# Order of work in a fused mLSTM and gated MLP kernel: the plan of the second product's steps, the place of the decay, and the joins of the first chunk

## The chip, the cores and the metric

The kernel runs on one core of a Trainium2 chip. The metric is the device time of one execution in microseconds. A core has TensorE (PE, matmuls; PEld is its weight load), VectorE (DVE), ScalarE (ACT), GpSimd (POOL) and SyncE (SP, which issues nearly all transfers here). Each works through its own queue in order; semaphores tie the queues together.

## The reference

An mLSTM cell runs over 768 time steps for 4 batches of 8 heads with a head dimension of 40. Its output, 3072 tokens of 320 values, goes through a two-layer block with a gate `h cos(h)`.

```python
# for each step t, with m the running maximum of the gates
C = f_stab * C + i_stab * outer(v_t, k_t)
n = f_stab * n + i_stab * k_t
y_t = sigmoid(o_t) * (C @ q_t) / max(|n . q_t|, 1)
# x = y as (3072, 320)
h = x @ w_in                     # w_in 320 x 2048
out = (h * cos(h)) @ w_out       # w_out 2048 x 320
```

## The kernel before

**Tiles.** Time is cut into 6 chunks of 128 steps. A cell `n` is one batch of one chunk (24 cells, `c, b = divmod(n, 4)`). A cell computes decay exponents E (8 heads of 128 x 128), scores, weighted scores, values, and a normalized result that is written transposed into xT. A chunk of xT, 512 tokens over the four batches, then goes through w_in.

**The loop.** `both_parts(c, b)` (line 976) runs the MLP of chunk c beside cell `n = 4(c + 1) + b`, the next chunk's cell of the same batch. It holds two *slots*, `8c + 2b` (first half) and `8c + 2b + 1` (second half). Each slot makes one `Up` (line 617): 8 + 4 matmul instructions into two PSUM tiles, then per tile `near` (ScalarE, line 639), `rest` (VectorE, line 642), `sin` (ScalarE, line 647) and `gate` (VectorE, lines 654 and 659). `ps_u` has two buffers, both used by one Up: the next Up can't begin before the gates have read the last one's tiles. In the first half the cell's scores, weighing, values and normalizing lie around the Up, in the second half the seam (the transposes of the result or, in later chunks, the state's product) and the state.

**w_out.** In chunk 0 `down_first(p)` (line 823) multiplies directly. From chunk 1 on a *step* `(c, s, p, parted)` adds piece p (of 8) to the sums of half s of chunk c. A parted step (`in_parts`, line 729) makes seven products P1 to P7 of 128 x 160 from sums of gate tiles, `S` (GpSimd, line 723), and differences of w_out, `T` (line 696); a whole step (`whole`) makes eight matmul instructions of 128 x 320. The step with p = 7 ends a sum: `put_together` (one ScalarE copy and seven VectorE ops, lines 759 and 765), or `whole_out` (two copies, line 752), and then the result transfers. `plan` (lines 679 to 690) is a hand-written table that says in which slot each step runs; `down(T)` (line 783) carries out a slot's steps, whole ones first, and `sums(T)` makes their S a slot ahead. The sums lie in `ps_o`, four PSUM banks in turn; a group takes three (`sums_room`, line 773), and (1,0) and (1,1) together four.

**Order on the engines.** The program order is written out by hand (`manual_schedule`), and each engine keeps it. The lines that the change and the prediction touch:

- `decay_exponents(n)` (373): VectorE subtraction (375) and GpSimd select (376); `decay(n)` (384): ScalarE's exponential. The exponential and the sine need different tables; `sin_next` (963) runs the sine on one element, so that its table is loaded early.
- `parts` and `join` (132, 143): the weights arrive as 64-bit floats. `parts` makes two ScalarE passes (138, 140) into the buffers wt and wm, two of each in turn; `join` makes three VectorE ops (144, 146, 148) and an integer add (149), on GpSimd or, in the first cells, on VectorE. In chunk 0 each block joins three pieces of w_in for the next block and two pieces of w_out.
- `turn_blocks(n)` (414): VectorE's 32 x 32 transposes, for cells from `TURNED = 7` on; before that TensorE turns (`turn`).
- `values_turned`, `normalize_turned` (490 to 522): PSUM tiles hp in `ps_a`, two buffers; VectorE's line 519 reads them, and the second half's `seam` (596) takes the same buffers.
- `first_cells` (839): gates and the first four cells, and the first w_in pieces.

In the first half of a block with c > 0 the program order before the change is: Up, scores, near, rest, weigh, rest, sin and gate twice, decay_exponents(n + 1), then (for a slot that ends a sum) the steps with put_together, then decay(n + 1), values, normalize. The second half: sin_next, sums, Up, seam, near, rest, sin and gate, state, the slot's steps, turn_blocks of the next cell.

Of the kernel before, what the change touches and what calls it, by code (L numbers as in the profile page):

```python
# [29 lines left out]
def kernel(  # L30
# [22 lines left out]
    B, H, S, D = q.shape  # L53
    C = 128
# [328 lines left out]
    def decay(n):  # L383
        nc.scalar.activation(out=Es[n], in_=Es[n], func=AF.Exp, scale=-1.0)  # L384
# [294 lines left out]
    def put(T, *steps):  # L679
        plan.setdefault(T, []).extend(steps)  # L680

    for p in range(NP):
        put(9 + p, (1, 0, p, IN_PARTS))
        put((9, 11, 13, 15, 17, 17, 18, 18)[p], (1, 1, p, WHOLE))
        put((19, 19, 20, 21, 21, 22, 23, 24)[p], (2, 0, p, IN_PARTS))
        for c in range(2, NC):
            if c > 2:
                put(8 * c + 5 + p // 2, (c, 0, p, IN_PARTS))
            put(8 * c + 9 + p // 2, (c, 1, p, WHOLE if c == NC - 1 and p == NP - 1 else IN_PARTS))
# [39 lines left out]
    def in_parts(c, s, p):  # L729
        P1, P2, P6, P5, P3, P4, P7 = po[c, s]  # L730
        g, S, T = gs[c, p, s], sg[c, s, p], Ts[p]
        w0, w1 = (w_out_sb[:, 2 * p + e] for e in range(2))
        last = p == NP - 1 or (c, s, p + 1, WHOLE) in plan[LAST]

        for out, a, w, first in ((P1, g[:, 0:C], w0[:, lo], True), (P2, g[:, 2 * C:3 * C], w1[:, lo], False),
                                 (P6, S[:, 1], T[:, 1], False), (P7, S[:, 2], T[:, 2], c > 1),
                                 (P5, S[:, 0], T[:, 0], True), (P3, S[:, 3], w1[:, hi], False),
                                 (P4, g[:, 3 * C:4 * C], T[:, 3], False)):
            product(out, a, w, first and p == 0, last)

    def whole(c, s, p, b, sums, alone=False):
# [8 lines left out]
    def whole_out(c, b, sums):  # L750
        o = p2.tile([128, DM], FP, name="o_sb", tag="o_sb")
        nc.scalar.copy(out=o, in_=sums)
        result(c, b, o)
# [19 lines left out]
    def sums_room(c, s):  # L773

        t = [ps_o.tile([128, 3 * DH + 32], FP, name="po", tag="o") for _ in range(3)]
        po[c, s] = [t[i // 3][:, ts(i % 3, DH)] for i in range(7)]
        if c == 1:

            t.append(ps_o.tile([128, 3 * DH + 32], FP, name="po", tag="o"))
            po[c, s][6] = t[2][:, DM:DM + DH]  # L780
            po[c, 1] = [x[:, 0:DM] for x in t[2:]]

    def down(T):

        rests = []
        steps = sorted(plan[T], key=lambda step: (step[3], step[:3]))
        for c, s, p, parted in steps:
            if p == 0 and (c, s) not in po:
                sums_room(c, s)
        for c, s, p, parted in steps:  # L790
            end = p == NP - 1
            if parted:
                in_parts(c, s, p)
                if end:
                    o2 = put_together(c, s)
                    rests.append(lambda c=c, s=s, o2=o2: [result(c, 2 * s + b, o2[:, b]) for b in range(2)])
            else:
                for b in range(2):
                    whole(c, s, p, b, po[c, s][b])
                if end:  # L800
                    rests.append(lambda c=c, s=s: [whole_out(c, 2 * s + b, po[c, s][b]) for b in range(2)])
            spare.append(gs.pop((c, p, s)))
        return rests

# [34 lines left out]
    def first_cells():  # L839
        nc.vector.memset(nil, 0.0)  # L840
        gates_in()
        nc.scalar.copy(out=ident_b, in_=ident)
        load(0, "qk")
        later_gates_in()
        load(1, "qk")
        load(0, "v")
        load_o(0, (0, 1))
        load(2, "qk")
        load_E(0)
        load_E(1)  # L850
        warm(7)
        gates_first()
        later_fills()
        wall_in(0, 0, pmu)
        wall_in(0, 1, psum_o())
        spread(0, 0)
        gates_first_out()
        decay_exponents_half(0, 0)
        turn(0)
        turn_out(0, False)  # L860
        gates_sums()
        spread(0, 1)
        decay_exponents_half(0, 1)
        decay(0)
        weigh_k(0)
        load_E(2)
        load(1, "v")
        load(3, "qk")
        load(2, "v")
        load_E(3)  # L870
        load_o(0, (2, 3))
        load(3, "v")
        pieces.extend(weights_in(0))
        wall_in(1, 0, psum_o())
        wall_in(1, 1, psum_o())
        gates_less_sums()
        spread(1, 0)
        decay_exponents_half(1, 0)
        scores(0)
        gates_maxima()  # L880
        turn(1)
        weigh(0)
        turn_out(1, False)
        sigmoid(0, slice(0, 2))
        spread(1, 1)
        decay_exponents_half(1, 1)
        gates_exponents()
        decay(1)
        weigh_k(1)
        values(0)  # L890
        normalize(0)
        scores(1)
        turn(2)
        turn_out(2, False)
        warm(2)
        seam(0)
        weigh(1)
        seam_out(0)
        state(0)
        load_E(B)  # L900
        load(B, "qk")
        decay_exponents(2)
        decay(2)
        weigh_k(2)
        gates_exp()
        values(1)
        outs.append((0, weights_out(0)))
        load(B, "v")
        load_o(1, (0,))
        load_E(B + 1)  # L910
        normalize(1)
        scores(2)
        turn(3)
        seam(1)
        weigh(2)
        turn_out(3)
        seam_out(1)
        decay_exponents(3)
        gates_diagonal()
        values(2)  # L920
        decay(3)
        weigh_k(3)
        state(1)
        scores(3)
        weigh(3)
        pg = gates_turn()
        warm(5)
        values(3)
        join(*parts(*pieces.pop(0)))
        sigmoid(0, slice(2, 4))  # L930
        gates_keep(*pg)
        pieces.extend(weights_in(1))
        load(B + 1)
        outs.extend((p, weights_out(p)) for p in range(1, 3))
        load_o(1, (1, 2, 3))
        normalize(2)
        warm(5)
        seam(2)
        seam_out(2)
        second = parts(*pieces.pop(0))  # L940
        normalize(3)
        warm(4)
        seam(3)
        join(*second, nc.vector)
        decay_exponents(B)
        seam_out(3)
        join(*parts(*pieces.pop(0)), nc.vector)
        load_E(B + 2)
        state(2)
        state(3)  # L950

        nc.scalar.activation(out=spot, in_=spot, func=AF.Exp)
# [23 lines left out]
    def both_parts(c, b):  # L976
# [25 lines left out]
        up.rest(1)  # L1002
        if c == 0 and not begin:
            weigh(n)
        if begin:
            decay_exponents(n + 1)
        for e in range(2):
            up.sin(e)
            up.gate(e)
        if more and c > 0:  # L1010
            decay_exponents(n + 1)
        if n == TURNED:
            turn_gates(n)
# [7 lines left out]
        if pieces:  # L1021
            h = parts(*pieces.pop(0))
        rests = []
        ends = any(step[2] == NP - 1 for step in plan.get(slot, ()))
        if ends:
            rests = down(slot)
        if begin or more and c > 0:
            decay(n + 1)
        elif more:
            decay_by_bias(n + 1)  # L1030
        if 0 < slot <= NP:
            down_first(slot - 1)
# [4 lines left out]
        if cell:  # L1037
            if n < TURNED:
                load(n + 2)
                if not begin:  # L1040
                    values_kept(n)
                values(n)
                normalize(n)
                if h:
                    join(*h)
            else:
                values_turned(n)
                if h:
                    join(*h)

                normalize_turned(n)
                if n + 2 < N:
                    load(n + 2, "q")
                last_in(n)
                if n + 2 < N:
                    load(n + 2, "bkv")
            if TURNED <= n + 2 < N:
                load_G(n + 2)
            if n + 3 < N:
                load_E(n + 3)  # L1060
            if b == B - 2 and c + 2 < NC:
                load_o(c + 2)
            fade(n)
            if n + 1 == TURNED:
                turn_blocks(n + 1)
        h = ()
        sin_next()
        if pieces:
# [10 lines left out]
            seam_out(n)  # L1079
        if cell and n < TURNED:  # L1080
            state(n)
        if h:
            join(*h)
        for e in range(2):
            up.sin(e)
            up.gate(e)
        if n >= TURNED and cell:
            state(n)
        if b == B - 1 and 0 < c < NC - 2:
            sigmoid(c + 2)  # L1090
            sin_next()
        if more:
            weigh_k(n + 1)
        if c == 1 and b < B - 1:
            two_differences(2 * b + 2)
        if pieces:
            join(*parts(*pieces.pop(0)))
        if c == 0:
# [67 lines left out]
```

## Time and profile before

| | |
|---|---|
| median of 3 runs | 537.48 us (532.47, 537.48, 537.7) |
| the profiled execution's own time | 532.62 us |
| its span in the profile | 530.9 us |
| TensorE busy | 518.6 us |
| VectorE busy | 404.5 us |
| ScalarE busy | 264.7 us |
| GpSimd busy | 210.0 us |
| TensorE's idle time in 40 to 120 us | 3.0 us (80.00 less 76.99) |
| TensorE's idle time in 208 to 222 us | 0.7 us (14.00 less 13.32) |
| TensorE's idle time in 265 to 300 us | 1.7 us (35.00 less 33.26) |

Times in the profile are microseconds from the start of the span. A row of a timeline gives start, duration, engine, line, operation, output and inputs, and how many instructions it merges; in brackets stands the idle time before it and what ended it. Chunk 0's blocks run from about 36 us (slot 0) to 128 us, slot 1 begins at 47.5, slot 2 at 59.2, slot 4 at 83.3, slot 6 at 107.0. Slot 16 begins at 204.8, slot 18 at 224.4, slot 24 at 280.8. An idle time counts toward the end only if the engine is the bound at that place.

### The profile page before, as it was taken

Reading aid. Unit: us, or ns where it says so; the run is one execution under the profiler, and the core shown is the slowest. Engines: PE = TensorE matmul, PEld = TensorE weight load, DVE = VectorE, ACT = ScalarE, POOL = GpSimd, SP = SyncE. Lnnn points to the kernel's source line nnn. Section 1 sums busy time; section 2 is a strip of 40 time slices with the busy share of each in tenths; the row PEclk is TensorE's granted clock in tenths of the full one; section 3 lists DMA queues with packets and bytes.
Section 4 is the critical chain, followed back from the end, with each engine's and each line's share of the span. In section 5 each row is a group of like instructions: output and inputs, shape, how many; then the busy total and the mean of one; then the engine's idle time right before and its main releaser. Section 6 shows DMA issues by size and latency. Waiting matters only on the chain.

```text
span 530.9 us, 10605 instructions
## 1 busy us (share of the span) xinstructions
PE 518.6 (98%) x3855; PEld 343.8 (65%) x3855; DVE 404.5 (76%) x864; ACT 264.7 (50%) x418; POOL 210.0 (40%) x409
## 2 busy tenths in 40 slices
PE   9999999999999999999999999999999999999996
PEld 6865566655565656556665577577577576757596
DVE  5878768889789998978999988988878864325253
ACT  3789696766543637543556363356353332313210
POOL 6522433333827532122521643532533524344350
PEclk9999999999999999999999999999999999999999
DMA  9989998932463475356276355366354100000000
GB/s 139 217 205 240 221 237 183 212 77 66 130 143 73 97 150 116 111 123 146 54 148 147 83 118 116 85 136 143 86 107 83 41 11 29 2 1 26 0 27 25
DMA packets 134860, 57.80 MB, mean 109 GB/s; under 512 B 70248, under 2 KB 130872, under 8 KB 134808
## 3 DMA queue, kind: packets, MB, share of 16 engines
q1 hardware_dynamic: 134664, 56.93, 48.2%
q8 instruction: 30, 0.49, 0.4%
q0 software_dynamic: 96, 0.18, 0.2%
q14 instruction: 22, 0.18, 0.1%
q10 hardware_dynamic: 48, 0.02, 0.0%
HBM read 50.76 MB, written 6.34 MB: 108 GB/s over the span
## 4 chain that ended last, share of the span: by engine, by line
PE 73%; DVE 8%; SPq 6%; ACT 6%; DMA 4%; issue 2%; POOL 0%; DVEq 0%; ACTq 0%; POOLq 0%
PE po L727 29%; PE pup L631 26%; PE pup L634 8%; SPq L332 4%; PE hp L496 3%; PE po L823 3%; PE ps L453 2%; DMA bits<-in_moe_w_in_dram 2%; PE hp L490 2%; DVE n L642 1%; SPq L129 1%; DMA qs<-in_q_dram 1%; PE pu L596 1%; ACT n L639 1%; ACT wt L138 1%
## 5 line engine op out<-in xcount | busy, mean ns | idle before, releaser
L631 PE MATMUL pup<-xT,w_in_sb 128*128 128x512 f32 x384 | 175.4, 599 | 3.2 <-DVE g L654 1.8
L639 ACT ACTIVATE n<-pup 128x512 int32<-128x512 f32 x96 | 51.8, 590 | 149.0 <-PE pup L634 149.0
L642 DVE SCALAR_TENSOR_TENSOR n<-pup,n 128x512 f32<-128x512 f32 x96 | 63.2, 685 | 80.0 <-ACT n L639 79.7
L631 PEld LDWEIGHTS pup<-xT,w_in_sb 128*128 128x128 f32 x384 | 69.6, 190 | 76.8 <-issue 65.5
L647 ACT ACTIVATE n<-n 128x512 f32<-128x512 f32 x96 | 59.5, 631 | 41.1 <-DVE n L642 41.1
L376 POOL TENSOR_SCALAR_AFFINE_SELECT E<-E 128x1024 f32<-128x1024 f32 x19 | 20.7, 1091 | 147.3 <-DVE E L375 139.8
L727 PE MATMUL po<-T,sg 128*128 128x160 f32 x426 | 69.4, 299 | 0.0
L727 PEld LDWEIGHTS po<-T,sg 128*128 128x128 f32 x426 | 61.7, 190 | 0.0
L634 PE MATMUL pup<-xT,w_in_l 64*128 64x512 f32 x192 | 54.7, 641 | 0.6 <-DVE w_in_l L149 0.6
L723 POOL TENSOR_TENSOR sg<-g 128x128 f32<-128x128 f32 x66 | 30.4, 460 | 53.6 <-PE po L727 40.9
L723 POOL TENSOR_TENSOR sg<-gg 128x128 f32<-128x128 f32 x66 | 30.6, 464 | 28.7 <-PE po L727 27.6
L634 PEld LDWEIGHTS pup<-xT,w_in_l 64*128 64x128 f32 x192 | 14.7, 184 | 37.2 <-issue 33.4
L384 ACT ACTIVATE E<-E 128x1024 f32<-128x1024 f32 x21 | 22.2, 1057 | 32.3 <-POOL E L376 28.6
L727 PE MATMUL po<-w_out_sb,g 128*128 128x160 f32 (+1 forms) x180 | 38.3, 341 | 0.0
L823 PE MATMUL po<-w_out_sb,g 128*128 128x320 f32 x128 | 36.6, 439 | 0.7 <-POOL w_out_sb L149 0.7
L414 DVE STREAM_TRANSPOSE t<-qs 128x512 f32<-128x512 f32 x34 | 35.1, 1112 | 0.4
L727 PEld LDWEIGHTS po<-w_out_sb,g 128*128 128x128 f32 x180 | 27.8, 189 | 11.0 <-issue 6.8
L727 PE MATMUL po<-w_out_sb,gg 128*128 128x160 f32 (+1 forms) x168 | 34.0, 329 | 0.0
L659 DVE SCALAR_TENSOR_TENSOR g<-pup,n 128x256 f32<-128x256 f32 x82 | 31.1, 417 | 2.1 <-ACT n L647 0.8
L459 DVE TENSOR_TENSOR E<-ps,E 128x512 f32<-128x512 f32 x48 | 30.7, 680 | 2.5 <-ACT E L384 2.1
L453 PEld LDWEIGHTS ps<-t,t 40*128 40x128 f32 (+1 forms) x384 | 25.4, 188 | 9.5 <-issue 8.9
L659 DVE SCALAR_TENSOR_TENSOR gg<-pup,n 128x256 f32<-128x256 f32 x78 | 29.8, 418 | 2.1 <-ACT n L647 1.2
(171 smaller groups left out, 854.1 us busy)
## 6 DMA issues: line engine op xcount, KB each, us to landing
E<-M_d SPq DMA_DIRECT2D x22, 512.0 KB
bits<-in_moe_w_in_dram SPq DMA_DIRECT2D x40, 128.0 KB
bits<-in_moe_w_out_dram SPq DMA_DIRECT2D x8, 640.0 KB
room<-G_d SPq DMA_DIRECT2D x34, 128.0 KB
ks<-in_k_dram SPq DMA_DIRECT2D x24, 160.0 KB
vs<-in_v_dram SPq DMA_DIRECT2D x24, 160.0 KB
out_dram<-o SPq DMA_DIRECT2D x18, 160.0 KB
o<-in_o_gate_dram SPq DMA_DIRECT2D x68, 40.0 KB
```

The lines of the kernel that those rows point to most:

```text
L414: nc.vector.transpose(out=dst.rearrange("r p (t x) -> r p x t", x=T4), in_=src.rearrange("r p (x d) -> r p x d", x=T4)[:, :, :, 0:32])
L453: nc.tensor.matmul(ps[j][:, p], kT[r, p], qT[r, p], start=True, stop=True)
L459: nc.vector.tensor_tensor(out=w, in0=pss[n][j], in1=w, op=OP.mult)
L631: nc.tensor.matmul(pu, w_in_sb[:, i, ts(block(f2, e), 128)], x(i), start=(i == 0), stop=False)
L634: nc.tensor.matmul(pu, w_in_l[r, f2], x(NK, r), start=False, stop=True)
L639: nc.scalar.activation(out=self.n[e], in_=self.pu[e], func=AF.Copy, bias=0.25)
L642: nc.vector.scalar_tensor_tensor(out=self.n[e].bitcast(FP), in0=self.pu[e], scalar=0.25, in1=self.n[e], op0=OP.add, op1=OP.subtract)
L647: nc.scalar.activation(out=r, in_=r, func=AF.Sin, scale=TWO_PI_DOWN)
L659: nc.vector.scalar_tensor_tensor(out=gs[c, f2, s][:, ts(e, W)], in0=self.pu[e][:, ts(s, W)], scalar=TWO_PI, in1=n[:, ts(s, W)], op0=OP.mul ...
L723: engine.tensor_tensor(out=S[:, i], in0=x, in1=y, op=op)
L727: nc.tensor.matmul(out, g, w, start=start, stop=stop, skip_group_check=True)
L823: nc.tensor.matmul(po[0][b], gs[0, f // 2, f % 2][:, ts(b, C)], w_out_sb[:, f], start=(f == 0), stop=(f == NF - 1))
```

## The change

Five edits; no arithmetic is altered.

1. The plan: whole step (1,1,7) moves from slot 18 to 19, and the steps of (2,0) shift, so that first halves (even slots) from 16 to 24 hold one step each and the second halves 17, 19, 21 and 23 hold two.
2. `in_parts` multiplies in the order P1, P2, P6, P5, P3, P4, P7, where P7 stood fourth. `sums_room` is called when a step needs it, not ahead of all of a slot's steps, and a whole sum's output copies follow at once.
3. `late`: in a block with c > 0 whose first half has a single step and that step ends a sum (slots 16 and 24), decay_exponents(n + 1) and decay(n + 1) move to the second half, behind the state, with one more `sin_next`.
4. Chunk 0: decay_exponents(n + 1) of the first block goes behind the gates; the second half's first join goes behind the gates; turn_blocks(7) goes from the end of a first half to the second half, between its two joins of w_in.
5. `first_cells`: decay_exponents(4) goes behind the third join of w_in.

```diff
-        put((9, 11, 13, 15, 17, 17, 18, 18)[p], (1, 1, p, WHOLE))
-        put((19, 19, 20, 21, 21, 22, 23, 24)[p], (2, 0, p, IN_PARTS))
+        put((9, 11, 13, 15, 17, 17, 18, 19)[p], (1, 1, p, WHOLE))
+        put((19, 20, 21, 21, 22, 23, 23, 24)[p], (2, 0, p, IN_PARTS))
...
-                                 (P6, S[:, 1], T[:, 1], False), (P7, S[:, 2], T[:, 2], c > 1),
-                                 (P5, S[:, 0], T[:, 0], True), (P3, S[:, 3], w1[:, hi], False),
-                                 (P4, g[:, 3 * C:4 * C], T[:, 3], False)):
+                                 (P6, S[:, 1], T[:, 1], False), (P5, S[:, 0], T[:, 0], True),
+                                 (P3, S[:, 3], w1[:, hi], False), (P4, g[:, 3 * C:4 * C], T[:, 3], False),
+                                 (P7, S[:, 2], T[:, 2], c > 1)):
...
         for c, s, p, parted in steps:
+            end = p == NP - 1
             if p == 0 and (c, s) not in po:
-                sums_room(c, s)
-        for c, s, p, parted in steps:
-            end = p == NP - 1
+                sums_room(c, s if c > 1 else 0)
...
-                    rests.append(lambda c=c, s=s: [whole_out(c, 2 * s + b, po[c, s][b]) for b in range(2)])
+                    for b in range(2):
+                        whole_out(c, 2 * s + b, po[c, s][b])
...
         join(*second, nc.vector)
-        decay_exponents(B)
         seam_out(3)
         join(*parts(*pieces.pop(0)), nc.vector)
+        decay_exponents(B)
...
-        if begin:
-            decay_exponents(n + 1)
         for e in range(2):
             up.sin(e)
             up.gate(e)
-        if more and c > 0:
+        ends = any(step[2] == NP - 1 for step in plan.get(slot, ()))
+        late = more and ends and len(plan[slot]) == 1
+        if begin or more and c > 0 and not late:
             decay_exponents(n + 1)
...
-        if begin or more and c > 0:
+        if begin or more and c > 0 and not late:
             decay(n + 1)
-        elif more:
+        elif more and c == 0:
             decay_by_bias(n + 1)
...
-            if n + 1 == TURNED:
-                turn_blocks(n + 1)
...
-        if h:
-            join(*h)
         for e in range(2):
             up.sin(e)
             up.gate(e)
+        if h:
+            join(*h)
         if n >= TURNED and cell:
             state(n)
+        if late:
+            decay_exponents(n + 1)
+            decay(n + 1)
+            sin_next()
...
         if c == 1 and b < B - 1:
             two_differences(2 * b + 2)
+        if n + 1 == TURNED:
+            turn_blocks(n + 1)
         if pieces:
             join(*parts(*pieces.pop(0)))
```

More of the change, by code (lines that the diff above doesn't have):

```diff
@@ L1023, in both_parts @@
         rests = []
-        ends = any(step[2] == NP - 1 for step in plan.get(slot, ()))
         if ends:
             rests = down(slot)
-        if begin or more and c > 0:
+        if begin or more and c > 0 and not late:
             decay(n + 1)
-        elif more:
+        elif more and c == 0:
             decay_by_bias(n + 1)
```

## The prediction

> **What bounds the kernel now.** I read the page first (busy shares), then the table by stretches of the span, then who waited for whom, then TensorE's timeline for its gaps, and last VectorE, ScalarE and GpSimd around each gap.
>
> ```profile
> span 530.9 us, 10605 instructions
> PE 518.6 (98%) x3855; PEld 343.8 (65%) x3855; DVE 404.5 (76%) x864; ACT 264.7 (50%) x418; POOL 210.0 (40%) x409
> ```
> ```profile
> 40.00:120.00 80.00, 76.99 (x456) 47.41 (x455) 65.00 (x125) 62.74 (x110) 28.47 (x30) 1.00 0.85 194
> 120.00:208.00 88.00, 88.00 (x677) 52.98 (x675) 80.08 (x157) 47.62 (x68) 43.54 (x79) 1.00 0.48 109
> 300.00:524.00 224.00, 224.00 (x1614) 156.01 (x1614) 145.93 (x337) 80.59 (x128) 90.33 (x198) 1.00 0.27 62
> ```
> The second number of a row is TensorE's busy time: from 120 to 208 us and from 300 to 524 us it has no gap, at a granted clock of 1.00. The change removes no matmul, so only gaps can be won. Those it aims at are these (bracket: idle time before, and who ended it):
>
> ```profile
> 41.13 1.13 PE L634 MATMUL pup<-xT,w_in_l 64*128 64x512 f32 x4 [0.55 <-DVE w_in_l L149]
> 47.52 3.70 PE L631 MATMUL pup<-xT,w_in_sb 128*128 128x512 f32 x8 [0.32 <-DVE g L654]
> 59.23 3.67 PE L631 MATMUL pup<-xT,w_in_sb 128*128 128x512 f32 x8 [0.66 <-DVE g L654]
> 65.08 4.57 PE L823 MATMUL po<-w_out_sb,g 128*128 128x320 f32 x16 [0.22 <-POOL w_out_sb L149]
> 83.32 3.67 PE L631 MATMUL pup<-xT,w_in_sb 128*128 128x512 f32 x8 [0.20 <-DVE g L654]
> 89.17 4.58 PE L823 MATMUL po<-w_out_sb,g 128*128 128x320 f32 x16 [0.23 <-POOL w_out_sb L149]
> 106.95 3.67 PE L631 MATMUL pup<-xT,w_in_sb 128*128 128x512 f32 x8 [0.62 <-DVE g L654]
> 112.79 4.57 PE L823 MATMUL po<-w_out_sb,g 128*128 128x320 f32 x16 [0.22 <-POOL w_out_sb L149]
> 219.43 0.51 PE L596 MATMUL pu<-vs,kw 128*40 128x41 f32 x16 [0.68 <-DVE room L519]
> 280.77 3.70 PE L631 MATMUL pup<-xT,w_in_sb 128*128 128x512 f32 x8 [1.17 <-DVE g L659]
> 295.88 0.51 PE L596 MATMUL pu<-vs,kw 128*40 128x41 f32 x16 [0.58 <-DVE room L519]
> ```
> The three L823 rows matter most for chunk 0: right behind the wait for a gate comes one for the joined piece of w_out. Two engines share the blame there, and shortening the first wait alone moves nothing. How that piece comes about in slots 3 and 4 (rows of GpSimd, ScalarE and VectorE):
>
> ```profile
> 82.62 1.27 POOL L149 TENSOR_TENSOR w_in_sb<-wt,wm 128x512 int32<-128x512 int32 x1 [3.28 <-DVE wt L148]
> 83.92 0.80 ACT L138 ACTIVATE wt<-bits 128x640 f32<-128x640 f32 x1 [2.37 <-POOL w_in_sb L149]
> 85.15 0.49 DVE L144 TENSOR_SCALAR wt<-wt 128x640 f32<-128x640 f32 x1
> 87.58 1.54 POOL L149 TENSOR_TENSOR w_out_sb<-wt,wm 128x640 int32<-128x640 int32 x1 [1.36 <-DVE wt L148]
> ```
> ScalarE's copy of the w_out piece waited 2.37 us for GpSimd's add of the w_in piece, whose buffers (two in turn) it takes.
>
> **The change, part by part** (times are those of the profiled execution).
>
> **Plan of w_out, chunk 2.** Same 28 steps, moved between slots. Up of slot 24 waited 1.17 for slot 23's gates, because one step (2.10) lay between Up 23 and it; now two lie there (4.00, from the two-step slots), 1.9 more, so 1.17 goes and some 0.7 is left over. What pays is slot 18, with one whole step (eight matmuls, 2.27) instead of 4.5, and 20, 22 with one as before. In slot 18 the first gates ended 3.8 after the start of the ScalarE copy (229.03 to 232.8); scores 0.89, 2.27 and values 1.61 cover 4.77 after Up. No wait: 0. **Gain 1.17.**
>
> **Late decay** (one step that ends seven sums: slots 16 and 24). VectorE's subtraction E (213.97 to 215.10) stood before the seven ops of put_together and normalize; L519 freed the bank for the seam 0.68 and 0.58 late. E moves behind the state, 1.13 of VectorE, so L519 comes 1.13 earlier: both waits go. **Gain 0.68 + 0.58.** What queues behind it: on VectorE, turn_blocks starts at 224.46 as before. On GpSimd, the select moves with it, and in slot 25 the kw product and the eight sums of slot 26 stand behind it: select to 302.8, kw 0.72, then 0.46 each to 307.1, where TensorE wants the second step's first sum at 307.9. 0. On ScalarE, E's exponential waits for the select: select ends 225.77 (224.46 + lag 0.22 + 1.09), exponential, sine table and its one-element op took 2.54 from there to the next copy (216.38 to 218.92): 228.31; Up 18 wants it at 228.35 (229.03 less 0.68). In slot 26: 305.29 against 304.51, 0.8 late, where the gates have 2.6 to spare (308.9 to 311.50). 0, bounds -0 and +0.4 (one more table load of 1.28 in front, less the 0.9 to spare in slot 18). The two added one-element ops (0.20) run while ScalarE idles: 0. No transfer moves here.
>
> The Trainium skill, "ScalarE: Activation LUTs", section "What ACT_TABLE_LOAD costs", speaks against this part: it puts a switch at 2.66 us, 1.28 of load and 1.38 of drain. The row of the sine's load here is 1.28 (217.52) and the next op starts 0.01 later, so no drain shows; by the page the copy of slot 18 would be 1.3 late, 0.44 of it on TensorE, and the sum below would be 0.44 higher. I take the row.
>
> **P7 last, sums_room later, whole_out at once.** Same matmuls. S[2] is needed 0.8 later, S[0], S[3] and P4's g 0.3 earlier; no L727 matmul waits in the trace, and sums lie a slot ahead. In slot 19 P7 needs the bank of the first output copy: copies 0.73 for two right after the whole step, P7 comes 1.8 after it. The two result transfers (160 KB each) move by a slot, past one block's loads on SP; SP waited 15.7 for all such copies without holding TensorE. Were ScalarE busy at that moment, P7 would wait for the copies alone, 0.73. I take 0.
>
> **First cells.** E(4), 1.13 on VectorE, moves behind the third join: w_in_l is ready 2.4 earlier (a neighbouring GpSimd select and kw stretched L146 to 1.07 there), so 0.55 goes. E(4)'s select then ends about 41.1, and its exponential started at 41.51 for ScalarE's own queue: 0. In slot 0 E(5) goes behind the gates: 0.32 goes. TensorE is 0.87 earlier into slot 1, but ScalarE, which sets slot 1 (its copy at 54.24 came 2 us behind Up), only 0.34, the wait it had for VectorE at 45.17.
>
> **Chunk 0, joins behind the gates.** VectorE's steps by start to start, slot 3: rest 1.21, state 0.69, join 1.65, gates 1.21, second join 1.46, w_out join 2.28, then GpSimd 1.69 with lag. Old order: 78.93 to 89.12. New: gates 80.83, join 82.04 to 83.66, GpSimd's add ends 85.10 instead of 83.89, ScalarE's copy 85.13 to 85.93, so the w_out join starts at 85.97 instead of 85.15: the gates no longer lie over that chain, only the second join does. Cost 0.82 at 89.17, less some 0.1 of GpSimd overlap: **+0.7**. Slot 2, the same less the 0.34: **+0.3**; and there Up also waits about 1 us for w_in_sb, so 0.66 isn't won. The w_out join also issues the transfer of the piece three further on, as much later; that piece is turned into floats a block on: 0. Slots don't add: ScalarE's copy at 70.75 waited for a DMA, which anchors slot 3.
>
> Slot 5: TensorE comes 0.7 late, ScalarE's copy at 101.64, rest at 102.25 instead of 102.63 (turn_blocks, 1.94, no longer before it). But turn_blocks now stands between the joins: -0.38 + 1.94 - 0.2 (no GpSimd neighbour for L146) = **+1.35** at 112.79. That replaces the +0.7, and since TensorE has no gap behind 118 it stays to the end. Bounds: -2.35 (all of 0.55, 0.32, 0.66, 0.20, 0.62 won) and +4.0 (the three add up, 0.82 + 0.82 + 1.26, and L146 stretched from 0.70 to 1.07 three times).
>
> **Sum:** -1.17 - 0.68 - 0.58 + 1.35 = -1.08. The profiled execution took 532.62 (span 530.9 and 1.7 around it): **531.5**. The three runs shown are 537.48, 532.47, 537.7; the profiled one is like the lowest, the median 4.86 above. Two of three stood above, so I forecast the median there: 537.48 - 1.08 = **536.4**.
>
> **Rivals.** (1) Everything is won: the copy of the w_out piece doesn't come later, chunk 0 loses all five waits: -2.43 - 2.35 = -4.78, 532.7 on the median. For it: VectorE idles 2.6 to 2.75 before each odd slot's rest. Against: the 2.37 wait above. (2) Slower: in chunk 0 each later GpSimd add hands its delay on, w_in buffer to ScalarE copy to w_out join to L823. At +4.0 the whole is +1.6, 539.1; it decides once chunk 0 costs over 2.43. For it: three L823 rows already wait for GpSimd. Against: the anchor at 70.75. (3) The change wins nothing late: the bank or ScalarE holds slots 17 to 26 as before, only 1.17 comes: +0.2, 537.7. Against: 1.13 moved exceeds both waits.
>
> **How the numbers follow.** Chances: forecast 0.52, (1) 0.20, (2) 0.18, (3) 0.10. About 1% (5.4 us) is what a measurement of this kernel can tell from no change, and no case reaches it alone; the level of the runs can. A median that falls on the lower level (0.3) with a gain is 531.5 or less, faster by over 1%: 0.3 x 0.72, with 0.05 for a gain I don't see: 0.27. Slower by over 1% needs a chunk 0 cost of 7.8 or a wait that the trace doesn't show: 0.13. Within: 0.60. Range: from (1) on the lower level, 527.8 (given as 528), to (2) on the upper with 1 us for a wait not seen, 540.
>
> **What would show it.** Right: no wait before the seams of slots 17 and 25 and before Up 24; E and its select behind the state in slots 17 and 25 only; ScalarE's copy of slot 18 within 0.2 of Up's end; L823 of slots 2, 4 and 6 waiting 0.7 to 1.0 for w_out_sb instead of 0.22, the last of them about 1.3 later; Up 2 waiting for w_in_sb. Wrong: those L823 no later than before (then rival 1), a gap behind 118 us, or a wait of Up 19 for gates.

## The result and the profile after

| | before | after |
|---|---|---|
| median of 20 runs | 533.09 us (531.52 to 537.7) | 531.35 us (529.09 to 536.19) |
| ratio, 95% interval | | 0.9963, 0.994 to 0.9986 |
| profiled execution, span | 532.62, 530.9 us | 532.54, 530.8 us |

The changed kernel is faster by 0.37% (0.14 to 0.6%): about 2.0 us of 533.09, between 0.75 and 3.2. That is within 1%. The forecast gain of 1.08 lies in that interval; the forecast time, 536.4, is 5.0 above the measured median.

The two profiled executions took nearly the same time, for reasons that cancel. The start of each Up on TensorE, from the two timelines, shows it:

| from, to | before | after | difference |
|---|---|---|---|
| span's start to Up 0 | 36.03 | 37.56 | +1.53 |
| Up 0 to Up 7 (chunk 0) | 82.88 | 83.87 | +0.99 |
| Up 7 to Up 27 | 192.52 | 189.99 | -2.53 |
| Up 27 to the last matmul | 215.40 | 215.40 | 0.00 |

The first row comes from a clock that sank before any edited code ran: from 14 to 16 us the two are level to 0.03, by 19 us the changed one is 1.55 behind (more below). The second and third are mainly the change: dearer in chunk 0, cheaper behind it; both hold waits for transfers too, which vary from execution to execution. First the page of the changed kernel and its table by stretches (TensorE's busy time is the second number of a row).

```profile
span 530.8 us, 10591 instructions
PE 519.4 (98%) x3855; PEld 345.3 (65%) x3855; DVE 406.9 (77%) x864; ACT 264.5 (50%) x420; POOL 212.9 (40%) x409
```
```profile
40.00:120.00 80.00, 75.86 (x411) 46.49 (x417) 66.31 (x121) 62.02 (x108) 29.61 (x30) 1.00 0.85 192
120.00:208.00 88.00, 88.00 (x736) 53.68 (x721) 79.22 (x158) 47.18 (x71) 43.37 (x78) 1.00 0.46 106
208.00:222.00 14.00, 14.00 (x133) 8.13 (x131) 12.16 (x31) 5.20 (x10) 0.68 (x2) 1.00 0.56 141
265.00:300.00 35.00, 35.00 (x319) 23.14 (x318) 32.28 (x74) 18.65 (x27) 11.33 (x22) 1.00 0.59 137
```
From 208 to 222 and from 265 to 300 us TensorE has no gap left (0.7 and 1.7 before). From 40 to 120 us its idle time rose from 3.0 to 4.1. Its timeline says where:

```profile
62.49 1.98 PE L631 MATMUL pup<-xT,w_in_sb 128*128 128x512 f32 x4 [1.50 <-POOL w_in_sb L149]
...
67.38 4.57 PE L825 MATMUL po<-w_out_sb,g 128*128 128x320 f32 x16 [0.88 <-POOL w_out_sb L149]
...
91.07 4.58 PE L825 MATMUL po<-w_out_sb,g 128*128 128x320 f32 x16 [0.27 <-POOL w_out_sb L149]
...
112.42 1.13 PE L634 MATMUL pup<-xT,w_in_l 64*128 64x512 f32 x4 [0.62 <-POOL w_in_l L149]
...
115.31 4.57 PE L825 MATMUL po<-w_out_sb,g 128*128 128x320 f32 x16 [0.87 <-POOL w_out_sb L149]
...
221.59 0.51 PE L596 MATMUL pu<-vs,kw 128*40 128x41 f32 x16
...
281.64 3.60 PE L631 MATMUL pup<-xT,w_in_sb 128*128 128x512 f32 x8
...
295.99 0.51 PE L596 MATMUL pu<-vs,kw 128*40 128x41 f32 x16
```
No Up of chunk 0 waits for gates any more. The waits come back one step on, for joined pieces: of w_in in the Ups of slots 2 and 6, of w_out (line 825 now) in slots 2, 4 and 6. The last three rows, the seams of slots 17 and 25 and Up 24, have no bracket: the waits of 0.68, 0.58 and 1.17 are gone.

### The profile page after: what moved, and what is told of

It is laid out like the page before. It is cut to its first block, busy times and chain, and to the rows that moved or that the text cites. A ratio compares the mean times of both kernels' runs of the same rounds, so it can differ in the third digit from the quotient of the medians.

```text
span 530.8 us, 10591 instructions
## 1 busy us (share of the span) xinstructions
PE 519.4 (98%) x3855; PEld 345.3 (65%) x3855; DVE 406.9 (77%) x864; ACT 264.5 (50%) x420; POOL 212.9 (40%) x409
## 4 chain that ended last, share of the span: by engine, by line
PE 82%; SPq 7%; DVE 4%; DMA 2%; ACT 2%; POOL 1%; issue 1%; DVEq 0%; POOLq 0%; ACTq 0%
PE po L727 30%; PE pup L631 28%; PE pup L634 9%; PE po L825 4%; SPq L332 3%; PE hp L496 3%; PE ps L453 3%; PE hp L490 2%; PE pu L596 1%; DVE wt L148 1%; SPq L306 1%; SPq L301 1%; DVE wt L146 1%; DMA E<-M_d 1%; SPq L129 1%
## 5 line engine op out<-in xcount | busy, mean ns | idle before, releaser
L727 PE MATMUL po<-T,sg 128*128 128x160 f32 x426 | 81.1, 299 | 0.0
L727 PEld LDWEIGHTS po<-T,sg 128*128 128x128 f32 x426 | 65.5, 190 | 0.0
L723 POOL TENSOR_TENSOR sg<-gg 128x128 f32<-128x128 f32 x66 | 31.8, 481 | 32.1 <-PE po L727 31.2
L453 PEld LDWEIGHTS ps<-t,t 40*128 40x128 f32 (+1 forms) x384 | 26.7, 193 | 9.2 <-issue 8.4
```

The costliest lines, as they stand in the source:

```text
L453: nc.tensor.matmul(ps[j][:, p], kT[r, p], qT[r, p], start=True, stop=True)
L723: engine.tensor_tensor(out=S[:, i], in0=x, in1=y, op=op)
L727: nc.tensor.matmul(out, g, w, start=start, stop=stop, skip_group_check=True)
```

## The experiments

All are timed against the kernel before on the chip; "Up 0 to Up 7" and "Up 7 to Up 27" are from each one's profile. Chunk 0 isn't independent of when Up 0 starts: in most profiles where that was early (34.2 to 36.0), ScalarE's pass over a w_in piece near 70 us waited for its transfer, 0.48 to 1.72; in the changed kernel, e1 and e6 (37.5 to 37.6) it didn't. So chunk 0 is compared between like starts.

| kernel | Up 0 at | Up 0 to Up 7 | Up 7 to Up 27 | ratio, 95% interval |
|---|---|---|---|---|
| before | 36.03 | 82.88 | 192.52 | 1 |
| after | 37.56 | 83.87 | 189.99 | 0.9963, 0.994 to 0.9986 |
| e1, later edits alone | 37.64 | 82.26 | 189.35 | 0.9947, 0.9927 to 0.9967 |
| e2, chunk 0's edits alone | 34.15 | 84.75 | 192.90 | 1.0038, 1.0011 to 1.0066 |
| e3, own buffers | 35.27 | 84.60 | 189.12 | 0.9946, 0.993 to 0.9962 |
| e4, turn back | 34.63 | 84.51 | 189.12 | 0.9956, 0.9939 to 0.9973 |
| e5, one add on VectorE | 41.94 | 83.10 | 189.10 | 0.9981, 0.9954 to 1.0007 |
| e6, three adds on VectorE, turn back | 37.53 | 81.42 | 189.29 | 0.9936, 0.9915 to 0.9957 |
| e7, plan and order alone | 42.04 | 81.88 | 192.13 | 0.9988, 0.9957 to 1.002 |
| e8, late decay alone | 35.69 | 82.28 | 190.96 | 0.9987, 0.9959 to 1.0016 |
| e9, old order, three adds on VectorE | 34.88 | 85.79 | 189.34 | 0.9962, 0.9939 to 0.9985 |
| e10, old order, w_out's add on VectorE | 34.37 | 83.59 | 189.42 | 0.9944, 0.9916 to 0.9971 |

**e1: the later chunks' edits alone** (1 to 3; edits 4 and 5 undone).

```diff
...
-        for e in range(2):
-            up.sin(e)
-            up.gate(e)
         if h:
             join(*h)
+        for e in range(2):
+            up.sin(e)
+            up.gate(e)
...
```


> The changed kernel with all edits of chunk 0 and of the first cells undone; plan, late decay, order of P7 and the room for sums stay. Measure: on TensorE, the start of Up 7 less the start of Up 0 (82.88 before, 83.87 in the changed kernel) and the start of Up 27 less that of Up 7 (192.52 before, 189.99 changed). Theory A (the later chunks win 2.5, chunk 0 pays 1.0 back): 82.9 and 190.0, some 2.5 us faster than before, ratio 0.9953, so faster than the full change. Theory B (chunk 0's edits win too, and the 1.0 seen there came from the changed kernel's late start in that one profile, 37.56 instead of 36.03 for Up 0): the same two spans, but slower than the full change, ratio 0.997 to 0.999.

Up 7 to Up 27 is 189.35, 3.17 less than before, where the prediction had 2.43. Chunk 0 is 1.61 shorter than the changed kernel's at the same start (37.64 and 37.56): that is the price of its edits.

**e2: chunk 0's edits alone** (4 and 5 in the kernel before).

```diff
...
+        for e in range(2):
+            up.sin(e)
+            up.gate(e)
         if h:
             join(*h)
-        for e in range(2):
-            up.sin(e)
-            up.gate(e)
...
```


> The kernel before with only the edits of chunk 0 and of the first cells. Theory A: Up 0 to Up 7 83.9 (1.0 more than before), Up 7 to Up 27 192.5 as before; 1.0 us slower, ratio 1.002, and the copies of the w_out pieces on ScalarE wait 3 us for GpSimd's add of w_in. Theory B: Up 0 to Up 7 82.9 or less with a start like that of before, ratio 1.000 or below.

Slower: 0.38% (0.11 to 0.66), some 2 us. The same waits stand in the profile as after: 1.50 for w_in_sb in Up 2, and 0.88, 0.88 and 0.87 for w_out_sb in slots 2, 4 and 6 (after: 0.88, 0.27, 0.87). So the change joins a gain of about 0.5% (e1) with a loss of about 0.4%; the product of the two ratios, 0.9985, lies within the changed kernel's interval.

**e3: two more buffers for the first join.** It tells the predicted cause (ScalarE's pass waits until GpSimd's add frees wt and wm) from others.

```diff
...
-            h = parts(*pieces.pop(0))
+            own = [spare.pop(0) for _ in range(2)]
+            h = parts(*pieces.pop(0), own)
...
+            spare.extend(own)
```


> The changed kernel, but the second half's first w_in piece of chunk 0 takes two free gate tiles for its two ScalarE passes instead of the two turning buffers, so that the w_out piece's copy no longer waits for GpSimd's add. Theory A, buffer chain: L138's waits for GpSimd (10.8 us in all in the changed kernel) go, the w_out matmuls of slots 2 and 4 stand as far behind Up 0 as before the change (29.1 and 53.1, against 29.8 and 53.5 in the changed kernel); slot 6 keeps some 0.8 of turn_blocks between the joins: Up 0 to Up 7 83.7. Rival (VectorE's order itself costs it, not the buffer): slots 2 and 4 stay at 29.8 and 53.5, Up 0 to Up 7 83.9.

ScalarE's wait is gone, and chunk 0 is no shorter: 84.60, like e2 and e4. The w_out product of slot 2 starts 29.81 behind Up 0, where the changed kernel has 29.82. Slot 1 in rows of ScalarE, VectorE and GpSimd, first of the changed kernel, then of e3 (its L141, L149, L151 and L152 are L138, L146, L148 and L149):

```profile
56.29 1.29 DVE L642 SCALAR_TENSOR_TENSOR n<-pup,n 128x512 f32<-128x512 f32 x2 [2.40 <-ACT n L639]
...
61.18 1.26 POOL L149 TENSOR_TENSOR w_in_sb<-wt,wm 128x512 int32<-128x512 int32 x1 [4.90 <-DVE wt L148]
61.24 1.34 DVE L146 TENSOR_SCALAR wt<-wt 128x256 int32<-128x256 int32 x1
62.40 0.77 POOL L397 TENSOR_TENSOR kw<-ks,tab 128x320 f32<-128x320 f32 x1
62.47 0.80 ACT L138 ACTIVATE wt<-bits 128x640 f32<-128x640 f32 x1 [3.55 <-POOL w_in_sb L149]
62.62 0.83 DVE L148 SCALAR_TENSOR_TENSOR wt<-bits,wt 128x256 int32<-128x256 int32 x1
...
63.37 0.48 DVE L144 TENSOR_SCALAR wt<-wt 128x640 f32<-128x640 f32 x1
...
65.79 1.54 POOL L149 TENSOR_TENSOR w_out_sb<-wt,wm 128x640 int32<-128x640 int32 x1 [1.35 <-DVE wt L148]
```
```profile
54.01 1.29 DVE L645 SCALAR_TENSOR_TENSOR n<-pup,n 128x512 f32<-128x512 f32 x2 [2.38 <-ACT n L642]
...
56.55 0.77 ACT L141 ACTIVATE wt<-bits 128x640 f32<-128x640 f32 x1
...
58.89 1.26 POOL L152 TENSOR_TENSOR w_in_sb<-g,g 128x512 int32<-128x512 int32 x1 [4.89 <-DVE g L151]
58.96 1.35 DVE L149 TENSOR_SCALAR wt<-wt 128x256 int32<-128x256 int32 x1
...
60.34 0.82 DVE L151 SCALAR_TENSOR_TENSOR wt<-bits,wt 128x256 int32<-128x256 int32 x1
61.08 0.48 DVE L147 TENSOR_SCALAR wt<-wt 128x640 f32<-128x640 f32 x1
...
63.50 1.54 POOL L152 TENSOR_TENSOR w_out_sb<-wt,wm 128x640 int32<-128x640 int32 x1 [1.35 <-DVE wt L151]
```
With own buffers ScalarE's pass runs 2.3 ahead of GpSimd's add, and GpSimd's add of the w_out piece still starts 4.61 behind the w_in one's (58.89 to 63.50), as it does after (61.18 to 65.79). What the two kernels share is VectorE, which has no idle time from its `rest` (56.29 and 54.01) to the w_out piece's join (its first op at 63.37 and 61.08): 7.08 and 7.07 in all. On the way L146 on 128x256 starts 0.06 behind GpSimd's add, ends 0.14 behind it (62.58 against 62.44), and takes 1.34; L148, beside GpSimd's next op, takes 0.83. Before, the gates stood there (slot 1 of the kernel before, the same engines):

```profile
58.39 1.29 DVE L654 SCALAR_TENSOR_TENSOR g<-pup,n 128x512 f32<-128x512 f32 x2
58.53 1.27 POOL L149 TENSOR_TENSOR w_in_sb<-wt,wm 128x512 int32<-128x512 int32 x1 [3.89 <-DVE wt L148]
...
59.76 0.77 POOL L397 TENSOR_TENSOR kw<-ks,tab 128x320 f32<-128x320 f32 x1
...
59.98 0.70 DVE L146 TENSOR_SCALAR wt<-wt 128x256 int32<-128x256 int32 x1
...
60.72 0.42 DVE L148 SCALAR_TENSOR_TENSOR wt<-bits,wt 128x256 int32<-128x256 int32 x1
```
The gates took 1.29 beside the add, and 1.29 in the changed kernel (58.20) with GpSimd idle. In the kernel before, VectorE took 6.22 from `rest` to the w_out piece's join. So the buffers alone aren't the cause, and a new theory stands: gates run beside a GpSimd add unslowed, while the join's integer ops stand still. The old order had put the gates over the add.

The rows also show why removing one wait won nothing. In the changed kernel ScalarE's copy ends at 63.27 (62.47 and 0.80), 0.1 before VectorE comes to the same join at 63.37. Two chains, the buffers' and VectorE's, arrive together, and e3 shortened only the first.

**e4: turn_blocks(7) back at the end of the first half.**

```diff
+            if n + 1 == TURNED:
+                turn_blocks(n + 1)
         h = ()
...
-        if n + 1 == TURNED:
-            turn_blocks(n + 1)
         if pieces:
```


> The changed kernel with turn_blocks(7) back at the end of the first half of chunk 0's third block; joins stay behind the gates. Theory A: slots 2 and 4 as in the changed kernel (29.8 and 53.5 behind Up 0), slot 6's w_out matmuls at 77.3 instead of 77.75 (before: 76.76), Up 0 to Up 7 83.4. Rival (turn_blocks in the first half holds the gates, so putting it back costs 0.6): Up 0 to Up 7 84.4.

Chunk 0 is 84.51, beside 84.60 and 84.75 of e3 and e2: nothing won. In slot 5 of the changed kernel the transposes run beside the add, in 2.06 (2.06 in e5 too, where no add runs there), and then L146 takes 0.29 (1.34 in e4): they take the gates' old place as a cover. The 1.94 that the prediction charged is real as VectorE's time and nearly repaid in the same slot.

**e5: the add behind the gates on VectorE**, so that none runs on GpSimd beside the second join.

```diff
         if h:
-            join(*h)
+            join(*h, nc.vector)
```


> The changed kernel, but the add that ends the second half's first join in chunk 0 (behind the gates) runs on VectorE instead of GpSimd; the two turning buffers as in the changed kernel. After the run with own buffers moved nothing (w_out matmuls of slot 2 29.82 behind Up 0, as in the changed kernel), theory A2: VectorE's next join stands still beside GpSimd's add (L146 on 128x256 1.34 instead of 0.29 alone, L148 0.83 instead of 0.42). Expected by A2: L146 0.3 to 0.7 there, the second join 1.1 to 1.5 instead of 2.45, w_out of slot 2 at 29.1 to 29.3, Up 0 to Up 7 83.3 to 84.0 with an early start (84.6 with own buffers). Rival (the order on VectorE alone, without contention): the longer add on VectorE comes on top, w_out of slot 2 at 29.8 to 30.4.

L146 is back at 0.30 and L148 at 0.42 in slot 1, and the w_out product of slot 2 starts 28.78 behind Up 0 instead of 29.82: 1.04 sooner (0.09 of it was there in slot 1, at this late start). In slot 4 it is 1.38 sooner (52.13 against 53.51). In slot 5, where turn_blocks now has no add to cover, slot 6 waits 1.36 for w_in_l instead of 0.62, and 0.77 is left (76.98 behind Up 0 against 77.75). The shorter add also frees the buffers earlier, so this run shortens both chains, not VectorE's alone. The time alone couldn't tell: this profile, and 0.9981 with an interval to 1.0007, show no clear gain.

**e6: all three adds of a second half on VectorE, turn_blocks back.**

```diff
...
-            join(*h)
+            join(*h, nc.vector)
...
-            join(*parts(*pieces.pop(0)))
+            join(*parts(*pieces.pop(0)), nc.vector)
...
-            out_join(*h)
+            out_join(*h, nc.vector)
```


> The changed kernel with turn_blocks(7) back in the first half and all three adds of a second half of chunk 0 (two w_in pieces and the w_out piece) on VectorE. By A2 no VectorE op stands still, and the w_out piece's add takes 0.8 on VectorE instead of 1.54 with lag 0.15 on GpSimd: w_out matmuls of slot 2 at 28.2 to 28.6 behind Up 0, Up 0 to Up 7 82.0 to 82.6 with an early start, ratio 0.991 to 0.993, better than the later chunks' edits alone. Rival (VectorE is the bound of chunk 0 whatever the neighbour): 84 or more, ratio 0.995.

The same joins in slot 1, VectorE:

```profile
61.00 0.69 DVE L149 CUSTOM_DVE_ANT_0 w_in_sb<-wt,wm 128x1024 uint16<-128x1024 uint16 x1
61.61 0.28 DVE L144 TENSOR_SCALAR wt<-wt 128x256 f32<-128x256 f32 x1
61.93 0.30 DVE L146 TENSOR_SCALAR wt<-wt 128x256 int32<-128x256 int32 x1
62.26 0.42 DVE L148 SCALAR_TENSOR_TENSOR wt<-bits,wt 128x256 int32<-128x256 int32 x1
62.82 0.43 DVE L149 CUSTOM_DVE_ANT_0 w_in_l<-wt,wm 128x512 uint16<-128x512 uint16 x1
...
63.68 0.49 DVE L146 TENSOR_SCALAR wt<-wt 128x640 int32<-128x640 int32 x1
```
Three adds (0.69, 0.43, 0.82) came onto VectorE, and L146 fell from 1.34 to 0.30 and, on the w_out piece, from 0.90 to 0.49; GpSimd had taken 1.26, 0.84 and 1.54 for the same adds. Chunk 0 is 81.42, below the range expected: 2.45 less than the changed kernel and 0.84 less than e1, all three at one start. The ratio, 0.9936, is just above the one expected. Its median of 529.44 is the lowest of all, and its interval excludes the kernel before; it overlaps those of the changed kernel and of e1, so against them only the profiles speak.

**e7: e1 without the late decay**, that is the plan and the order of products.

```diff
...
-        late = more and ends and len(plan[slot]) == 1
+        late = False
...
```


> The kernel before with the new plan, the order of P7, the room for sums and the output copies at once; no late decay, chunk 0 as before. If the terms are apart: Up 24 without its wait for gates (1.17), the seams of slots 17 and 25 still 0.6 late: Up 7 to Up 27 191.2 to 191.4 (192.52 before; 189.1 with the late decay). If the late decay also hastens the transfer that the first Up of a chunk waits for, the difference between this and 189.1 is over 1.26.

Up 24 no longer waits, but Up 7 to Up 27 is just 0.39 shorter than before, where 1.1 to 1.3 was expected. The slots (table below) say why: slot 16 took 1.57 more, held by a transfer, of which slot 17 gave 0.60 back; slots 18, 19, 23 and 24 together are 1.82 shorter; and the seam of slot 25 waits 1.04 for L519, 0.46 more than before. So the plan does its part, and without the late decay VectorE takes a quarter of it back. Slot 16's delay came ahead of every moved step; whether it belongs to this kernel or to this execution is open.

**e8: the late decay alone**, in the kernel before.

```diff
...
+        if late:
+            decay_exponents(n + 1)
+            decay(n + 1)
+            sin_next()
```


> The kernel before with only the late decay of slots 16 and 24; old plan, chunk 0 as before. Seams of slots 17 and 25 without a wait, ScalarE's copy of slot 18 within 0.2 of the end of Up 18, Up 24 still 1.2 late: Up 7 to Up 27 190.7 to 191.3 (192.52 before).

Up 7 to Up 27 is 1.56 shorter (1.26 predicted): 0.75 in slot 17, 0.67 in slot 25, 0.10 in slot 26. No seam waits, and Up 24 still waits its 1.17.

**e9 and e10: the old order with adds on VectorE**: is it the order that wins in e6, or the adds?

```diff
...
-            out_join(*h)
+            out_join(*h, nc.vector)
```
This line, with chunk 0 and the first cells in the old order, is all of e10; e9 puts the two w_in adds on VectorE as well.

> The later chunks' edits alone (chunk 0 and first cells in the old order, first join ahead of the gates), with all three adds of a second half of chunk 0 on VectorE. It tells whether the gain of the run with the adds on VectorE and the joins behind the gates (Up 0 to Up 7 81.42) comes from the adds alone. Theory A2 with the order: the add (0.7) now stands before the gates too, so Up 2 waits for them some 1.3 instead of 0.65 and w_out of slot 2 stands at 29.2 to 29.7; Up 0 to Up 7 82.0 to 83.0, no better than with the adds on GpSimd (82.26). Rival (the adds alone): 81.2 to 81.7.

> The later chunks' edits alone, chunk 0 in the old order, with only the w_out piece's add in the second halves on VectorE (0.8 instead of 1.54 and 0.15 of lag on GpSimd). In the old order L823 of slot 2 waits 0.22 for that add, and before that Up 2 waits 0.65 for the gates. Expected: the 0.22 goes, L823 of slot 2 at 28.8 (29.02 with the adds on GpSimd), Up 0 to Up 7 81.7 to 82.1, and no more, since the waits for the gates stay. Rival: 82.3 or above, if VectorE's 0.8 delays the next slot's rest.

In e9 the gates stand behind a longer join, and Up 2, 4 and 6 wait for them 1.36, 2.42 and 1.49 (0.66, 0.20, 0.62 before): 85.79, the longest chunk 0 of all and 2.8 above the expected range. Part of that is probably the early start of 34.88, where ScalarE waits 1.72 for a piece's transfer. In e10 the wait of 0.22 for w_out_sb is gone, as expected, but Up 0 to Up 7 is 83.59: 1.5 above the expected range. The loss against e1 lies in one place, slot 3, where ScalarE waits 1.71 for the transfer and Up 4 then 1.70 for its gates: from slot 2's w_out product to slot 4's it is 25.29 against 23.50, from there to slot 6's 23.44 against 23.62. Its rival, a delay in every slot, would not look so. How both would do at a later start is open.

Slot 2's w_out product comes ahead of those waits, so its distance from Up 0 compares the kernels best:

| adds of the second half | old order | new order |
|---|---|---|
| all on GpSimd | 29.02 (e1) | 29.82 (after) |
| w_out's on VectorE | 28.75 (e10) | not run |
| first w_in piece's on VectorE | not run | 28.78 (e5) |
| all on VectorE | 29.45 (e9) | 28.52 (e6) |

Before and e8 agree with e1 to 0.03, and so do e2, e3 and e4 with after. e9 and e10 stand where they were expected (29.2 to 29.7, and 28.8). A late start alone can shift the figure: e7, with chunk 0 as before, has 28.64 at its start of 42.04, but it is 0.50 sooner than e1 in slot 1 already, where e5, at 41.94, is 0.09 sooner than after. So with all adds on GpSimd the new order loses 0.80, in the old order putting all adds on VectorE loses 0.43, and the two together win 0.50 over e1.

A third pair of wt and wm wasn't tried; e3 borrows tiles instead.

## Why the prediction came out as it did

Two steps failed. The level, "Two of three stood above, so I forecast the median there", put the forecast time, 536.4, above the kernel before (533.09 over 20 runs), while the changed kernel came out below it, at 531.35. And in chunk 0 "the gates no longer lie over that chain, only the second join does" took VectorE's ops at the same length in any order; the runs showed them 0.64 and 0.41 longer.

**Later chunks: right in place, 0.7 to 1.0 too small.** The three waits went and none took their place. The distance from each Up to the next on TensorE tells the parts (slots not shown differ by 0.1 or less):

| slot | before | after | e3 | e7, plan | e8, late |
|---|---|---|---|---|---|
| 16 | 9.19 | 9.57 | 9.19 | 10.76 | 9.19 |
| 17 | 10.29 | 9.54 | 9.54 | 9.69 | 9.54 |
| 18 | 11.59 | 9.44 | 9.44 | 9.44 | 11.59 |
| 19 | 9.04 | 9.32 | 9.31 | 9.37 | 9.03 |
| 23 | 8.46 | 9.03 | 9.04 | 9.04 | 8.46 |
| 24 | 9.77 | 9.66 | 9.18 | 9.19 | 9.72 |
| 25 | 9.70 | 9.03 | 9.04 | 10.15 | 9.03 |

In e3 the late decay's slots 17 and 25 are 1.41 shorter (1.26 forecast), the plan's 18, 19 and 23 together 1.30 (1.17 forecast), slot 24 0.59 and slot 26 0.10 (nothing forecast). Slot 18, the tight spot, went well: ScalarE's rows of the changed kernel in slots 17 and 18.

```profile
228.23 1.06 ACT L384 ACTIVATE E<-E 128x1024 f32<-128x1024 f32 x1 [2.62 <-POOL E L376]
229.31 1.28 ACT L967 ACT_TABLE_LOAD   x1
230.60 0.20 ACT L967 ACTIVATE spot<-spot 1x1 f32<-1x1 f32 x1
231.13 1.09 ACT L639 ACTIVATE n<-pup 128x512 int32<-128x512 f32 x2 [0.32 <-PE pup L634]
```
ScalarE is through with the sine's table 0.33 before Up hands it the copy (bracket: 0.32 of idle, ended by TensorE). The load took 1.28, with the next op 0.01 behind it, so the row was the right choice: the 2.66 of the Trainium skill, "ScalarE: Activation LUTs", section "What ACT_TABLE_LOAD costs", shows nowhere here.

Slot 24's 0.59 was in no gap. Before, its last w_in product waited inside a busy stretch: its rows, then the same of e3.

```profile
284.40 1.18 PE L634 MATMUL pup<-xT,w_in_l 64*128 64x512 f32 x3
285.37 0.27 PE L453 MATMUL ps<-t,t 40*128 40x128 f32 x1
285.42 0.59 PE L634 MATMUL pup<-xT,w_in_l 64*128 64x512 f32 x1
```
```profile
283.20 1.13 PE L637 MATMUL pup<-xT,w_in_l 64*128 64x512 f32 x4
284.17 1.06 PE L456 MATMUL ps<-t,t 40*128 40x128 f32 x16
```
Four instructions take 1.13 together; before, the group is spread over 1.61. It needs the last rows of xT, whose transfer SP issued at 281.76, 0.99 behind the start of Up 24; in e3 at 280.35, 0.67 behind it. The twelve profiles agree: the group is whole in the seven where the issue comes 0.05 to 0.67 behind that start, and spread in the five where it comes 0.90 to 1.43 behind (before, after, e1, e2, e8). In e7 the same kind of wait, in slot 16, has a name:

```profile
214.92 0.69 PE L634 MATMUL pup<-xT,w_in_l 64*128 64x512 f32 x1 [0.46 <-DMA xT<-X_d]
```
"The change removes no matmul, so only gaps can be won" was thus not exact. The changed kernel's profile still has 0.48 of it in slot 24 and 0.38 in slot 16, hence 2.53 there against 3.1 to 3.4 in e1, e3, e4, e5, e6, e9 and e10. All three profiles with the old plan have it in slot 24, two of nine with the new one, so the plan may have a part in it; how much belongs to the execution is open.

**First cells: right.** The waits of 0.55 and 0.32 are gone (no bracket after); Up 1 begins 10.46 behind Up 0, against 11.49 in e1: 1.03, where 0.87 was forecast. Of the 0.34 that ScalarE was to be earlier in slot 1, only 0.06 reached VectorE's `rest` (18.73 behind Up 0, 18.79 in e1).

**Chunk 0: right in sign, place and about in size; of the cause it saw one half.** Predicted were +0.3 in slot 2, +0.7 in slot 4 and +1.35 at the end. At a like start the w_out products of slots 2, 4 and 6 come 0.80, 0.98 and 1.60 later than in e1 (29.82, 53.51, 77.75 behind Up 0 against 29.02, 52.53, 76.15). They wait 0.88, 0.27 and 0.87 where 0.7 to 1.0 was forecast for each.

The chain that was predicted is there: in slot 1 the copy of ScalarE ends 6.97 behind `rest`, 5.80 in e1, so 1.17 later (1.21 forecast). The step that failed is "the gates no longer lie over that chain, only the second join does" with "less some 0.1 of GpSimd overlap". It charged VectorE's second join at 1.46 as before; the join took 2.45, because L146 went from 0.70 to 1.34 and L148 from 0.42 to 0.83 beside GpSimd's ops. VectorE so reaches the w_out piece's join 7.08 behind `rest` (6.22 in e1), 0.1 after the copy's end. e3 took the copy's wait away and the 7.08 stayed: VectorE's chain alone is enough. ScalarE's alone would hold the join nearly as long, but that is an estimate from its 6.97; no run has the short ops together with the add on GpSimd and the old buffers. That the cost forecast for slot 3 (0.82) and the measured one (7.09 less 6.22, 0.87) agree is luck: the chain that was missed happens to be as long as the one that was seen.

A stretch by GpSimd was in the prediction: the row of 1.07 for L146 in first_cells went into the 0.55 and the upper bound, and 0.1 and 0.2 were taken off for it elsewhere; in slots 1 and 3 it was put at nothing. In slot 2 the 0.34 (0.06 measured) went wrong as well, hence 0.80 instead of 0.3. The price of turn_blocks, 1.94 in the sum, was too high: e4 has nothing to win. The misses, too small and too large, offset each other. That the slots don't add held, though the transfer that was to anchor slot 3 held nothing up in this profile.

The Trainium skill, "SBUF — State Buffer", section "Who interferes with whom", has VectorE and GpSimd share one pair of ports, which one instruction holds to its end; it puts single-input forms like L146's on the list of those that can contend and exempts ops with at most one input from on-chip memory outside the two-port modes. The rows agree: 0.30 became 1.34 beside an add of 1.26, and the gates, with one input in PSUM, stayed at 1.29. That ports are the means is the page's statement; the runs show the lengths.

**Rivals.** Rival 1's chunk 0 (all five waits won) didn't come: with VectorE's joins behind the gates and no GpSimd add beside them, e6 gets 0.84 of its 2.35 against e1. Rival 2's condition, over 2.43, wasn't met: 1.6. Rival 3 is out.

**The level.** The forecast took 537.48 for the kernel before, the median of three runs; over 20 runs it is 533.09. Of the 5.0 by which the forecast missed, 4.4 lies there; the rest is the gain, which was put too small. Of 20 runs of before, two lie above 534.4 (537.48 and 537.7), and both were among the three shown; the profiled 532.62 was typical. The clock of those two is not on record; what may lie behind them shows in other runs' clocks: of the changed kernel's 20 runs the two with a mean granted clock under 0.99 (0.987 and 0.985) are the two slowest, 536.19 and 535.86; all others have 0.994 or more and 532.87 or less. A run of the kernel before at 0.987, timed beside e7, took 537.61; but another at 0.995 took 536.39, so the mean clock doesn't tell every such run. Where it goes, e7's profile shows (stretch, TensorE's busy time, and after the five engines the granted clock), beside before's:

```profile
32.00:40.00 8.00, 8.00 (x44) 5.74 (x43) 4.01 (x15) 3.66 (x8) 1.27 (x1) 0.50 1.02 216
```
```profile
32.00:40.00 8.00, 7.50 (x62) 4.28 (x60) 7.42 (x17) 6.88 (x18) 2.08 (x3) 1.00 0.85 192
```
At half the clock sixteen matmul instructions of L478 take 3.48 (1.88 before), and Up 0 starts at 42.04 instead of 36.03. The changed kernel's 1.53 is the same in small: 0.79 from 16 to 24 us, 1.00 there before.

## What to carry to other kernels

An op's duration can depend on its neighbour on another engine (here 0.30 or 1.34): when an order is changed, look up what ran beside each moved op, and keep the unslowed kinds (here gates and transposes) over GpSimd's adds, or take the adds off GpSimd. When a wait is removed and nothing is won, look for a second chain that ends at the same op: here two ended within 0.1 us. "No gap" doesn't mean "nothing to win": compare a group's merged count and length between slots to find a transfer's wait inside a busy row. And two of three runs at one level don't make that the kernel's level: here 18 of 20 lay with the third and with the profiled one.

## What was not expected of the hardware

- A GpSimd integer add of 128x512 (1.26) held a 128x256 VectorE op for its whole length, 1.34 in place of 0.30; VectorE did the same add, as an op on 16-bit halves, in 0.69, so where such an op lies over it, giving the add to GpSimd cost VectorE more than doing it.
- TensorE's granted clock sank to 0.50 (e5 and e7, 32 to 40 us) and 0.79 (after, e1, e5, e6 and e7, 16 to 24 us) in stretches in which it was busy for all 8.00 us, in some executions and not in others; e7's 6.0 us for the start are three times the whole effect of the change. Why is open.
